# Attention feeding an ELU feed-forward layer on one core: W1 loaded by column group, unit 1's v cast moved off GpSimd, units 4 and 5 turned by DMA

## The chip, the cores and the metric

The kernel runs on one core of a Trainium2 chip. The metric is device time in microseconds (us) of one execution. TensorE (PE) multiplies, VectorE (DVE), ScalarE (ACT) and GpSimd (POOL) do elementwise work, SyncE (SP) issues DMAs. POOL and ACT can issue DMAs too; a DMA issued by POOL runs in another queue (q0 in the profile) than one issued by SP (q1).

## The reference

Inputs are q, k and v of shape (8, 8, 576, 64), `w_in` (512, 2048) and `w_out` (2048, 512), all float32.

```python
q_s = softmax(q, axis=-1)            # over the 64 features of a row
k_s = softmax(k, axis=2)             # over the 576 positions
kv  = einsum('bhsd,bhse->bhde', k_s, v)
x   = einsum('bhsd,bhde->bhse', q_s, kv)      # -> (8*576, 8*64) = (4608, 512)
h   = x @ w_in                                # (4608, 2048)
g   = where(h > 0, h, exp(min(h, 0)) - 1)     # ELU
out = g @ w_out                               # (4608, 512)
```

## The kernel before

**Units and blocks.** The attention is cut into 16 units n: batch n // 2, and four of its eight heads. The rows of x are cut into 9 blocks j of 512 rows. For every block, GEMM1 (line 541) makes 2048 columns of h in 8 groups g of 256 (8 matmuls of 128x512 each, called H j.g here), the ELU makes G j.g from it, and GEMM2 (line 586) makes four output tiles ts of 128 rows (16 matmuls each; O j.ts[a:b] is a part of them). That is 576 + 576 matmuls.

**One unit.** Loads of q, k, v (576 KB each). `stage1`: exp of q and of k on ACT (lines 355, 359), cast of v to bf16 (line 363 on POOL or line 366 on ACT), then on DVE the row sums of exp q (371), their reciprocal (375) and the scaled QS (379). QS has to be turned: `tp` does it with 9 PE transposes (402) and a copy to qsT on ACT (409) or DVE (412); `turn` and `widen` do it with a DMA transpose issued by SP (418) into QT and an ACT copy to qsT (430). `kv_mm` is 36 small bf16 matmuls (454), for one unit or, with two columns of PSUM, for two units in a row; `m` divides by the sum of exp k (463) and writes MBLK (467). `ao_mm` (485) makes x transposed in two parts ao n.0 and ao n.1, and `xt` copies it into XT (507 on ACT, 510 on DVE). With `BYDMA = 6` units 0 to 5 go through `tp`; with `CASTS = 6` v of units 1 to 5 is cast on POOL.

**ELU.** ACT takes exp of a PSUM tile (557; E j.g). In blocks 0 and 1 odd groups take relu on ACT (568; R j.g) and one DVE operation (570); even groups, and all later ones, take two DVE operations (574 and 576). The result is GT. GEMM1 alternates between two PSUM tiles, so H j.(g+2) has to wait until G j.g was made.

**Order.** Operations are collected with their reads and writes, which give the semaphore waits. The order in which each engine issues its own operations is not planned at run time: it is written out as lists of operation numbers in `ORDER` (one list for each of PE, ACT, DVE, POOL and SP), and every engine keeps to its list. An operation that waits holds up everything behind it on its engine; a DMA that waits holds up every later DMA of its queue.

**Head.** SP loads q0, q1, k0, v0, k1, v1. POOL then loads W1 in six DMAs: 1024 columns in halves of the contraction (units 0, 1 give half each of it), then the other 1024 columns. The first of them waits for v0 (`gate`). The cast of v1 stands in POOL's list between the fifth and the sixth. W2 and the loads of units 2 to 5 follow on POOL. The matmuls of line 651 are fillers, which no result needs.

**Shared storage.** GT of block 1 lies over QS, qsT, v of odd early units and over block 0's output tiles OSBX (line 276), so G 1.6 and G 1.7 have to wait until the stores of block 0 have left. QT is a single buffer.

Decoded, the lists of before start like this (T = transposes on PE, vc = cast of v, ms = memset, D-transposes are `turn`):

```
PE   T0a kv0 T0b ao0.0 T1a T1b kv1 H0.0(half 0) ao1.0 H0.1(half 0) H0.0(half 1) ... H0.7 O0.0 O0.1 ...
ACT  expq0 expq1 expk0 vc0 expk1 qsT0a qsT0b qsT1a xt0.0 xt1.0 E0.0 E0.1 R0.1 E0.2 ...
DVE  ms ID, ms RZK, sum0 rec0 ms MBLK1, QS0, ms VB0, sum1 ms MBLK0, rz0 M0 ms VB1, rec1 M0 QS1 xt0.0 rz1 qsT1b M1 M1 xt1.0
POOL W1 x5, vc1, W1, W2.0 W2.1 q2 k2 v2 W2.2 q3 k3 v3 vc2 W2.3 q4 v4 vc3 q5 k4 vc4 v5 k5 vc5
SP   q0 q1 k0 v0 k1 v1, q6 st0.0 v6 st0.1 st0.0 st0.3 q7 st0.1 k6 k7 st0.3 st0.2 st0.2 v7 ...
block 1, PE   H1.0 H1.1 T4 H1.2 O1.1 O1.0 kv4 H1.3 ao4.0 ... ao4.1+kv5 H1.4 T5 ... ao5.1 H1.7 ... H2.0 ... H2.1 O1.0 kv6+kv7 O1.1 O1.2
block 1, ACT  expq4 .. expq5 E1.0 expk4 E1.1 R1.1 qsT4 E1.2 expk5 expq6 xt4.0 E1.3 xt4.1 R1.3 vc6 E1.4 qsT5 E1.5 R1.5 xt5.0 E1.6 expk6 E1.7 R1.7 expq7 expk7 xt5.1 vc7 E2.0 osb1.0 E2.1
```

Of the kernel before, what the change touches and what calls it, by code (L numbers as in the profile page):

```python
# [16 lines left out]
NU = 2 * B  # L17
CH = 9
BYDMA = 6
CASTS = 6  # L20
# [3 lines left out]
        "26 30 28 44 40 42 47 64 51 65 67 68 66 69 79 83 90 100 112 125 126 134 87 133 128 127 104 "  # L24
        "146 136 106 135 147 149 123 148 131 129 153 137 154 156 143 150 155 169 181 185 192 207 206 "
        "187 208 196 219 218 212 220 224 236 237 235 243 241 261 245 249 263 267 244 262 269 268 282 "
        "288 273 308 323 292 359 286 312 296 316 364 328 330 324 374 334 338 355 399 360 368 407 391 "
        "372 375 379 395 447 415 400 452 417 422 439 411 418 487 443 462 448 456 460 479 467 463 505 "
        "483 488 503 527 495 510 499 506 535 540 531 550 548 536 566 544 551 555 574 581 570 618 589 "
        "575 591 623 585 596 592 610 614 649 619 633 627 634 631 641 645 654 664 638 658 650 671 679 "  # L30
        "675 662 665 684 692 680 688 697 669 693 701 705 718 710 714 706 731 736 723 719 727 757 732 "
        "740 744 749 753 745 770 762 758 766 775 783 771 779 784 788 789 793 797 801 "),
    "act": (
        "3 20 31 21 22 32 27 29 41 45 52 70 73 74 76 80 81 84 91 92 101 94 113 88 114 95 89 105 116 "
        "124 117 130 132 157 173 166 144 151 160 163 198 170 174 182 183 186 193 199 226 197 209 213 "
        "210 228 221 225 238 239 242 246 227 264 265 252 253 250 254 270 289 283 309 251 293 349 287 "
        "301 299 313 297 298 329 317 331 321 325 300 320 335 365 339 356 348 361 404 382 369 373 384 "
        "408 392 376 380 381 433 396 383 405 401 416 432 423 470 412 453 419 440 444 449 457 461 480 "
        "472 464 469 492 468 484 493 489 504 471 496 521 511 500 528 520 507 541 532 559 537 558 560 "
        "549 545 552 557 582 605 571 556 567 579 590 576 580 624 586 597 593 604 615 611 620 628 632 "  # L40
        "635 642 646 659 655 651 640 672 639 676 666 663 681 685 689 698 702 694 711 707 715 737 720 "
        "670 728 733 724 741 750 754 746 759 763 767 772 776 780 785 790 794 798 802 804 "),
    "dve": (
        "0 2 23 24 7 25 4 34 5 37 38 6 35 39 36 46 48 43 49 50 53 71 72 75 77 78 82 85 86 93 102 97 "
        "103 98 99 115 119 120 107 108 109 121 138 139 140 145 152 176 177 178 201 171 172 184 188 "
        "194 189 190 202 195 203 214 215 216 211 222 223 229 230 240 231 247 248 266 255 256 257 271 "
        "272 274 284 275 276 277 278 279 285 294 295 302 303 314 315 304 350 318 319 351 326 327 336 "
        "352 337 340 357 358 341 362 342 363 343 344 370 345 371 385 386 377 378 387 434 397 402 398 "
        "435 424 403 425 426 473 413 414 436 427 428 474 420 429 421 445 446 450 451 458 475 459 465 "
        "466 490 485 486 491 522 512 513 523 501 514 524 515 502 508 516 509 517 533 534 538 539 561 "  # L50
        "546 547 553 554 572 562 573 563 577 606 578 598 587 599 588 607 594 595 616 600 601 608 602 "
        "603 617 621 622 629 630 647 648 636 637 660 661 652 653 677 678 667 668 682 683 690 691 703 "
        "695 696 704 708 709 716 717 721 722 729 730 734 742 743 735 755 747 748 756 760 761 768 769 "
        "773 774 781 782 "),
    "gp": (
        "1 14 15 16 17 18 33 19 54 55 56 57 58 59 60 61 62 96 63 110 122 118 141 111 175 180 142 200 "),
    "sp": (
        "8 9 10 11 12 13 179 159 205 162 158 168 204 161 191 217 167 165 164 234 233 232 260 259 310 "
        "280 311 291 258 307 290 281 305 333 347 306 322 366 346 332 354 353 409 390 388 393 389 367 "
        "394 431 441 406 455 437 410 438 478 454 430 476 442 482 494 519 518 481 477 529 497 525 498 "  # L60
        "526 565 530 542 584 568 543 569 625 564 609 583 626 612 643 644 613 656 673 657 674 699 686 "
        "687 700 712 738 726 713 739 725 777 778 751 752 764 765 795 786 787 791 796 792 800 803 799 "),
# [178 lines left out]
class Gen:  # L241
# [49 lines left out]
    def init(self):  # L291
        S = self.S
        S.add("dve", 100, lambda e: e.memset(self.ID[:, :], 0.0), -95, W=["ID"])
        S.add("gp", 300, lambda e: e.affine_select(
            self.ID[:, :], self.ID[:, :], compare_op=ALU.not_equal, fill=1.0, base=0,
            pattern=[[-1, 128]], channel_multiplier=1), -38, X=["ID"])
        self.ident = S.ops[-1]
        S.add("dve", 60, lambda e: e.memset(self.RZK[0][:, :], 0.0), -90, W=["RZK0"])
        S.add("act", 1400, lambda e: e.activation(self.RZK[0][:, :], self.RZK[0][:, :], AF.Exp), -80,
              X=["RZK0"])  # L300
        self.table = S.ops[-1]
        for i in range(2):
            S.add("dve", 150, lambda e, i=i: e.memset(self.VB[i][:, :, :, D:D + 1], 1.0), -8,
                  W=[f"VBone{i}"])
            S.add("dve", 300, lambda e, i=i: e.memset(self.MBLK[i][:, :, :].bitcast(F32), 0.0), -8,
                W=[f"MBLK{i}", f"MBLK{i}0", f"MBLK{i}1"])

    def load(self, n, t, key, eng="gp", follow=None):
# [6 lines left out]
        chain = eng == "gp" and n < 4  # L315
        S.add(eng, ISSUE[eng], lambda e: e.dma_start(dst, src), key, W=[name],  # L316
              dma=f"{name}{eng}", nbytes=128 * 4608, follow=self.gpq if chain else follow)
        S.ops[-1].margin = 400 if n < 4 else 1000 if n < 6 else 1500
        if chain:
            self.gpq = S.ops[-1]  # L320
# [7 lines left out]
    def load_w1(self, two, half, key, after=()):  # L328
        w = self.w_in.rearrange("(h kc d) f -> h d kc f", h=2, d=D)
        sl = slice(two * 1024, (two + 1) * 1024)  # L330
        ks = slice(0, 4) if half is None else slice(2 * half, 2 * half + 2)
        xs = (0, 1) if half is None else (half,)
        for h in range(2):
            self.S.add("gp", ISSUE["gp"], lambda e, h=h: e.dma_start(  # L334
                self.W1[h:128:2, ks, sl], w[h, :, ks, sl]), key,
                W=[f"W1_{s}{x}{h}" for x in xs for s in (2 * two, 2 * two + 1)],
                dma=f"w1{two}{xs[0]}{h}", nbytes=len(xs) << 19, after=after, follow=self.gpq)
            self.gpq = self.S.ops[-1]

    def load_w2(self, s, key, after=()):  # L340
# [4 lines left out]
        self.gpq = self.S.ops[-1]  # L345
        return self.gpq

    def stage1(self, n, key, vconv="gp", what="qk"):
# [8 lines left out]
        if "k" in what:  # L357
# [4 lines left out]
            if vconv == "gp":  # L362
                S.add("gp", 1053, lambda e: e.tensor_copy(  # L363
                    VB[:, :, :, 0:D], v[:, :, :, :]), key - 50, R=[vname], W=[f"VB{i}"])
            else:
                S.add("act", t_act(1152, False), lambda e: e.activation(  # L366
                    VB[:, :, :, 0:D], v[:, :, :, :], AF.Copy), key - 50, R=[vname], W=[f"VB{i}"])
            self.conv = S.ops[-1]
        if "q" not in what:
# [4 lines left out]
            key - 3, R=[f"qR{i}"], W=[f"ZQ{i}"])  # L374
# [69 lines left out]
    def kv_mm(self, n, ps, at=KV):  # L444
# [12 lines left out]
        return 510 if at == self.KV else 280, [f"kR{i}", f"VB{i}", f"VBone{i}"], mm  # L457
# [390 lines left out]
```

## Time and profile before

| | before |
|---|---|
| median of 13 runs | 305.58 us (305.18 to 307.09) |
| the profiled execution, its own time | 305.43 us |
| its span, first to last instruction | 303.6 us |
| PE busy | 288.3 us, 95% of the span |
| DVE, ACT busy | 189.5 us (62%), 180.6 us (59%) |
| POOL busy | 21.6 us (7%) |
| moved by DMA | 49.37 MB, 163 GB/s on the mean |

The span is what the rows of the profile lie in; 1.8 us of the execution's own time lie outside it. A row of the timeline is start, length, engine, line, operation, output<-inputs, shape and count; in brackets stands the idle time before it and what ended it. PE rows are pipelined: the length of a row overlaps the next one, so the cost of a piece of PE work is read from start to start. A matmul of 128x512 costs 0.227 us that way (16 of them from 106.11 to 109.74).

### The profile page before, as it was taken

Reading aid. Unit: us, or ns where it says so; the run is one execution under the profiler, and the core shown is the slowest. Engines: PE = TensorE matmul, PEld = TensorE weight load, DVE = VectorE, ACT = ScalarE, POOL = GpSimd, SP = SyncE. Lnnn points to the kernel's source line nnn. Section 1 sums busy time; section 2 is a strip of 40 time slices with the busy share of each in tenths; the row PEclk is TensorE's granted clock in tenths of the full one; section 3 lists DMA queues with packets and bytes.
Section 4 is the critical chain, followed back from the end, with each engine's and each line's share of the span. In section 5 each row is a group of like instructions: output and inputs, shape, how many; then the busy total and the mean of one; then the engine's idle time right before and its main releaser. Section 6 shows DMA issues by size and latency. Waiting matters only on the chain.

```text
span 303.6 us, 4456 instructions
## 1 busy us (share of the span) xinstructions
PE 288.3 (95%) x1875; PEld 234.9 (77%) x1875; DVE 189.5 (62%) x243; ACT 180.6 (59%) x210; POOL 21.6 (7%) x32
## 2 busy tenths in 40 slices
PE   0699999999999999999999999999999999999994
PEld 0577877778788888888888888878888888888883
DVE  2849854988959777598478657574755435644400
ACT  5658749998978859754975675634534234423411
POOL 0770235100000000000000000000000000000000
PEclk9999999999999999999999999999999999999999
DMA  7999997859677394837779122242020300200424
GB/s 268 367 377 393 390 383 250 282 143 304 182 225 217 121 332 119 219 73 203 197 226 314 45 96 56 54 92 54 17 52 0 71 17 17 69 2 0 104 54 119
DMA packets 32371, 49.37 MB, mean 163 GB/s; under 512 B 13920, under 2 KB 13920, under 8 KB 32352
## 3 DMA queue, kind: packets, MB, share of 16 engines
q1 hardware_dynamic: 27312, 33.50, 38.9%
q0 software_dynamic: 4960, 15.47, 15.3%
q8 instruction: 14, 0.23, 0.3%
q10 hardware_dynamic: 80, 0.13, 0.1%
q14 instruction: 5, 0.04, 0.0%
HBM read 36.70 MB, written 9.44 MB: 152 GB/s over the span
## 4 chain that ended last, share of the span: by engine, by line
PE 88%; DMA 6%; POOL 1%; DVE 1%; ACT 1%; SPq 0%; issue 0%
PE PS L586 42%; PE PS L541 41%; DMA W<-in_moe_w_in_dram 4%; PE PS L485 3%; DMA VR<-in_v_dram 2%; PE PS L454 2%; POOL W L334 1%; PE PS L402 1%; SPq L316 0%; DVE QS L379 0%; DVE GT L576 0%; POOL VB L363 0%; ACT ESB L557 0%; DVE MBLK L467 0%; DVE ESB L574 0%
## 5 line engine op out<-in xcount | busy, mean ns | idle before, releaser
L541 PE MATMUL PS<-XT,W 128*128 128x512 f32 x576 | 140.9, 393 | 0.9 <-ACT XT L507 0.6
L586 PE MATMUL PS<-W,GT 128*128 128x512 f32 x576 | 140.6, 392 | 0.0
L541 PEld LDWEIGHTS PS<-XT,W 128*128 128x128 f32 x576 | 106.2, 188 | 24.7 <-ACT XT L507 1.0
L586 PEld LDWEIGHTS PS<-W,GT 128*128 128x128 f32 x576 | 106.9, 188 | 22.5 <-ACT OSB L603 0.4
L557 ACT ACTIVATE ESB<-PS 128x1024 f32<-128x1024 f32 x72 | 73.6, 1027 | 69.2 <-PE PS L541 69.0
L574 DVE TENSOR_SCALAR ESB<-ESB 128x1024 f32<-128x1024 f32 x64 | 44.1, 691 | 66.4 <-ACT ESB L557 66.2
L576 DVE TENSOR_TENSOR GT<-ESB,PS 128x1024 fp32r<-128x1024 f32 x64 | 77.6, 1218 | 1.7
L603 ACT ACTIVATE OSB<-PS 128x512 f32<-128x512 f32 x32 | 19.0, 596 | 29.2 <-PE PS L586 20.7
L371 DVE TENSOR_REDUCE ZQ<-QR 128x18 f32<-128x1152 f32 x16 | 21.6, 1348 | 10.9 <-ACT QR L355 10.8
L507 ACT ACTIVATE XT<-PS 128x512 fp32r<-128x512 f32 (+6 forms) x32 | 19.4, 609 | 10.8 <-PE PS L485 10.6
L379 DVE TENSOR_TENSOR QS<-QR,RZQ 128x1152 f16<-128x1152 f32 x16 | 23.1, 1441 | 0.3
L355 ACT ACTIVATE QR<-QR 128x1152 f32<-128x1152 f32 x16 | 18.7, 1167 | 2.8 <-DMA QR<-in_q_dram 2.8
L359 ACT ACTIVATE KR<-KR 128x1152 bf16<-128x1152 f32 x16 | 18.5, 1161 | 0.7 <-DMA KR<-in_k_dram 0.7
L402 PE MATMUL PS<-ID,QS 128*128 128x128 f16 x54 | 4.7, 235 | 10.3 <-DVE QS L379 10.3
L485 PE MATMUL PS<-qsT,MBLK 128*128 128x320 f32 (+5 forms) x64 | 14.0, 306 | 0.0
L485 PEld LDWEIGHTS PS<-qsT,MBLK 128*128 128x128 f32 x64 | 11.5, 189 | 2.9 <-ACT XT L507 0.6
L366 ACT ACTIVATE VB<-VR 128x1152 bf16<-128x1152 f32 x11 | 12.8, 1164 | 0.3 <-DMA VR<-in_v_dram 0.3
L430 ACT ACTIVATE qsT<-QT 128x1152 fp32r<-128x1152 f16 x10 | 11.7, 1166 | 1.7 <-PE PS L454 1.7
L402 PEld LDWEIGHTS PS<-ID,QS 128*128 128x128 f16 x54 | 3.3, 104 | 11.8 <-DVE QS L379 10.7
L570 DVE SCALAR_TENSOR_TENSOR GT<-PS,ESB 128x1024 fp32r<-128x1024 f32 x8 | 9.8, 1224 | 3.1 <-ACT ESB L568 2.7
L467 DVE TENSOR_TENSOR MBLK<-PS,RZK 64x128 fp32r<-64x128 f32 x32 | 9.2, 288 | 0.8
L463 DVE RECIPROCAL RZK<-PS 128x2 f32<-128x2 f32 x16 | 2.6, 165 | 10.0 <-ACT XT L507 5.4
(27 smaller groups left out, 67.5 us busy)
## 6 DMA issues: line engine op xcount, KB each, us to landing
out_dram<-OSB SPq DMA_DIRECT2D x63, 128.0 KB, 2.4
QR<-in_q_dram SPq DMA_DIRECT2D x12, 576.0 KB, 4.4
KR<-in_k_dram SPq DMA_DIRECT2D x12, 576.0 KB, 5.0
VR<-in_v_dram SPq DMA_DIRECT2D x12, 576.0 KB, 4.2
W<-in_moe_w_out_dram POOLq DMA_DIRECT2D x4, 1024.0 KB, 14.6
QR<-in_q_dram POOLq DMA_DIRECT2D x4, 576.0 KB, 12.6
KR<-in_k_dram POOLq DMA_DIRECT2D x4, 576.0 KB, 11.4
VR<-in_v_dram POOLq DMA_DIRECT2D x4, 576.0 KB, 13.7
```

Of the source, the lines that this page charges most:

```text
L355: S.add("act", t_act(1152, False), lambda e: e.activation(flat(q), flat(q), AF.Exp), key - 3, X=[f"qR{i}"], follow=self.table)
L359: S.add("act", t_act(1152, False), lambda e: e.activation(ek[:, :, :, :].rearrange("p h c d -> p (h c d)"), flat(k), AF.Exp), key - 2, X=[ ...
L371: S.add("dve", t_dve(1152), lambda e: e.tensor_reduce(self.ZQ[i][:, :, :].rearrange("p h c -> p (h c)"), q[:, :, :, :].rearrange("p h c d ...
L379: S.add("dve", t_dve(1152), lambda e: e.tensor_tensor(qso, q[:, :, :, :], rz, ALU.mult), key - 3, R=[f"qR{i}", f"RZQ{i}"], W=[f"QS{self.al ...
L485: last = e.matmul(P[:, y:y + n_], M[:, f, :], T[:, c0:c1, f * 64:f * 64 + 64], start=True, stop=True)
L507: S.add("act", t_act((h1 - h0) * n_, True), lambda e, dst=dst, src=src: e.activation(dst, src, AF.Copy), key, W=W, X=X)
L541: last = e.matmul(P[:, t * 512:(t + 1) * 512], self.W1[:, kc, tt * 128:(tt + 1) * 128], self.XT[:, kc, rc:rc + BLK], start=(kc == 0), stop ...
L557: S.add("act", t_act(1024, True), lambda e: e.activation(esb[:, :], P[:, :], AF.Exp), key, W=[f"E{i}"], X=banks)
L574: S.add("dve", t_dve(1024, 2), lambda e: e.tensor_scalar(esb[:, :], esb[:, :], 1.0, -1.0, ALU.min, ALU.add), key, X=[f"E{i}"])
L576: S.add("dve", t_dve(1024), lambda e: e.tensor_tensor(gt, esb[:, :], P[:, :], ALU.max), key, R=[f"E{i}"], W=gw, X=banks)
L586: last = e.matmul(dst, GT[:, jj, ts * 128:(ts + 1) * 128], self.W2[:, jj, :], start=(jj == 0), stop=(jj == 15))
L603: S.add("act", t_act(512, True), lambda e: e.activation(osb[:, :], src, AF.Copy), key, W=[f"O{i}0", f"O{i}1"], X=[f"b{bk}"])
```

## The change

`load_w1` takes a range of groups: W1 comes in eight DMAs, groups 0 to 2 (768 columns) in two halves of the contraction, groups 3 and 4 (512 columns), groups 5 to 7 (768 columns). The first of them wait for k0 in place of v0 (`gate`). W2 no longer waits for the cast of v1. The cast of v1 is made of two halves, one on ACT (line 366's kind) and one on DVE. Memsets of VB and MBLK come first on DVE. With `BYDMA = 4` units 4 and 5 are turned by DMA and widened on ACT; with `CASTS = 4` their v is cast on ACT. k-v of units 4 and 5 is one pair. The first two groups of block 1's GEMM1 are issued in halves of the contraction. All five lists of `ORDER` are written anew. The diff without the lists:

```diff
-BYDMA = 6
-CASTS = 6
+BYDMA = 4
+CASTS = 4
+CAST0, CAST1 = "act", "split"
@@ init
         for i in range(2):
-            S.add("dve", 150, lambda e, i=i: e.memset(self.VB[i][:, :, :, D:D + 1], 1.0), -8,
-                  W=[f"VBone{i}"])
-            S.add("dve", 300, lambda e, i=i: e.memset(self.MBLK[i][:, :, :].bitcast(F32), 0.0), -8,
-                W=[f"MBLK{i}", f"MBLK{i}0", f"MBLK{i}1"])
+            S.add("dve", 80, lambda e, i=i: e.memset(self.VB[i][:, :, :, D:D + 1], 1.0), -88,
+                  W=[f"VBone{i}"], follow=S.ops[-1] if i else None)
+            S.add("dve", 280, lambda e, i=i: e.memset(self.MBLK[i][:, :, :].bitcast(F32), 0.0), -88,
+                  W=[f"MBLK{i}", f"MBLK{i}0", f"MBLK{i}1"], follow=S.ops[-1])
@@ load_w1
-    def load_w1(self, two, half, key, after=()):
+    def load_w1(self, g0, g1, half, key, after=()):
         w = self.w_in.rearrange("(h kc d) f -> h d kc f", h=2, d=D)
-        sl = slice(two * 1024, (two + 1) * 1024)
+        sl = slice(g0 * 256, g1 * 256)
...
@@ stage1
-            if vconv == "gp":
-                S.add("gp", 1053, lambda e: e.tensor_copy(
-                    VB[:, :, :, 0:D], v[:, :, :, :]), key - 50, R=[vname], W=[f"VB{i}"])
-            else:
...
+            for eng, h0, h1, x in {"gp": [("gp", 0, 2, "")], "act": [("act", 0, 2, "")],
+                                   "dve": [("dve", 0, 2, "")],
+                                   "split": [("act", 0, 1, ""), ("dve", 1, 2, "x")]}[vconv]:
...
@@ program
-            if (n, t) == (0, "v"):
+            if (n, t) == (0, "k"):
                 gate = S.ops[-1]
-        for two, half in ((0, 0), (0, 1), (1, None)):
-            self.load_w1(two, half, -30, [gate, self.ident] if (two, half) == (0, 0) else ())
+        for g0, g1, half in ((0, 3, 0), (0, 3, 1), (3, 5, None), (5, 8, None)):
+            self.load_w1(g0, g1, half, -30, [gate, self.ident] if half == 0 else ())
             S.ops[-2].behind = loaded
-        self.stage1(0, -8, vconv="act")
+        self.stage1(0, -8, vconv=CAST0)
-        self.stage1(1, -5)
+        self.stage1(1, -5, vconv=CAST1)
-        after = [self.conv]
-        self.load_w2(0, -29, after)
-        self.load_w2(1, -29, after)
+        self.load_w2(0, -29)
+        self.load_w2(1, -29)
...
+        def batch(b):
+            n = 2 * b
+            if b == 2:
+                yield from (first(n), loads(("v", n + 1), ("q", n + 2)), first(n + 1, "k"),
+                            loads(("v", n + 2)), wide(n), kv2(n), loads(("k", n + 2), ("k", n + 3)))
+            else:
+                yield from (first(n, "q"), loads(("q", n + 2)), wide(n))
...
+        for half in range(2):
+            for g in range(2):
+                self.hg_mm(1, g, 2 if g == 0 else g % 2, key, half)
         for g in range(8):
-            self.hg(1, g, 2 if g == 0 else g % 2, key, "da"[g % 2])
+            self.hg(1, g, 2 if g == 0 else g % 2, key, "da"[g % 2], g > 1)
```

The new lists, decoded in the same way (vcA, vcD are the halves on ACT and DVE):

```
PE   T0b T0a kv0 T1b T1a ao0.0 kv1 H0.0(half 0) ao1.0 H0.1(half 0) H0.0(half 1) ... H0.7 ao0.1+ao1.1 O0.1 O0.2 O0.3 O0.0 ...
ACT  expq0 expq1 expk0 vc0 qsT0b qsT0a expk1 vcA1 qsT1a xt0.0 xt1.0 E0.0 E0.1 R0.1 E0.2 ...
DVE  ms VB0, MBLK0, VB1, ID, MBLK1, RZK, sum0 rec0 QS0 sum1 rec1 QS1 rz0 M0 M0 vcD1 qsT1b xt0.0 rz1 M1 M1 xt1.0
POOL W1 x8, W2.0 W2.1 q2 k2 v2 q3 W2.2 W2.3 v3 k3 vc2 q4 v4 vc3 q5 k5 k4 v5
SP   q0 q1 k0 v0 k1 v1, st0.3 st0.0 q6 D-transpose4 v6 st0.1 D-transpose5 st0.2 st0.2 q7 v7 st0.0 st0.1 st0.3 k7 k6 q8 D-transpose6 ...
block 1, PE   H1.1, H1.0 (half 0), H1.0, H1.1 (half 1), H1.2 O1.1[0:2] O1.0[0:4] H1.3 O1.1[2:4] kv4+kv5 O1.1[4:6] H1.4 H1.5 O1.0[4:6] ao4.0 O1.1[6:8] H1.6 O1.1[8:10] ao4.1 H1.7 O1.0[6:8] ao5.0 O1.0[8:10] O1.1[10:12] O1.0[10:12] H2.0 O1.1 O1.0 H2.1 ao5.1+kv6+kv7 O1.2
block 1, ACT  expq4 osb0.2 osb0.3 xt3.0 xt3.1 vc4 expq5 E1.0 E1.1 R1.1 expk4 E1.2 vc5 expk5 E1.3 R1.3 widen4 E1.4 vc6 E1.5 R1.5 xt4.0 E1.6 xt4.1 widen5 E1.7 xt5.0 R1.7 expq6 vc7 expk7 expk6 osb1.0 E2.0 E2.1
block 1, DVE  sum4 rec4 QS4 m1.0 G1.0 G1.1 sum5 m1.2 G1.2 rec5 QS5 rz4 G1.3 M4 M4 rz5 M5 m1.4 M5 G1.4 G1.5 m1.6 G1.6 G1.7 sum6 ...
```

## The prediction

> **What bounds the kernel now.** I read the page's first and fourth part, then the chain of waits in order of time up to 60 us, then the timeline of its pieces.
>
> ```profile
> PE 288.3 (95%) x1875; PEld 234.9 (77%) x1875; DVE 189.5 (62%) x243; ACT 180.6 (59%) x210; POOL 21.6 (7%) x32
> ...
> PE 88%; DMA 6%; POOL 1%; DVE 1%; ACT 1%; SPq 0%; issue 0%
> ```
>
> PE is the bound: from its first GEMM matmul at 16.91 to its end it has hardly an idle row. The 1152 GEMM matmuls at 0.227 us (start to start, 16 of them from 106.11 to 109.74) are 261 us and are not touched. What can be won is the head before 16.91, other PE work, and restarts of PE.
>
> ```profile
> 2.27 6.93 DMA VR<-in_v_dram
> 9.20 0.30 issue
> 9.50 3.25 POOL W L334 x5
> 12.75 1.05 POOL VB L363
> 13.80 11.49 DMA W<-in_moe_w_in_dram
> 25.29 0.04 issue
> 25.33 7.55 PE PS L541 x32
> ```
>
> The chain says: v0 lands at 9.20, POOL issues five W1 loads, then casts v1, and only then issues the sixth, which lands at 25.29 and starts the second half of GEMM1. But PE idled just 0.15 us for it. The start at 16.91 has another cause, which the timeline shows:
>
> ```profile
> 12.49 2.64 DVE L379 TENSOR_TENSOR QS<-QR,RZQ 128x1152 f16<-128x1152 f32 x1
> 12.71 1.19 POOL L363 CAST VB<-VR 128x1152 bf16<-128x1152 f32 x1
> 15.18 0.68 PE L402 MATMUL PS<-ID,QS 128*128 128x128 f16 x9 [1.20 <-DVE QS L379]
> 15.67 0.70 ACT L409 ACTIVATE qsT<-PS 128x640 fp32r<-128x640 f16 x1 [2.70 <-PE PS L402]
> 16.27 0.59 ACT L507 ACTIVATE XT<-PS 128x512 fp32r<-128x512 f32 x1
> 16.91 1.19 PE L541 MATMUL PS<-XT,W 128*128 128x512 f32 x4 [0.64 <-ACT XT L507]
> ```
>
> QS of unit 1 takes 2.64 us beside POOL's cast, against 1.36 at 44.10, where POOL is idle; PE, then ACT, then the copy to XT follow one another. The DMA has a hole in the same place:
>
> ```profile
> 11.00:12.50 1.50, 1.50 (x44) 1.43 (x33) 0.95 (x6) 1.50 (x3) 1.50 (x3) 1.00 1.05 319
> ...
> 14.00:17.00 3.00, 1.18 (x46) 0.96 (x46) 2.49 (x4) 1.19 (x2) 3.00 (x5) 1.00 0.93 280
> 17.00:25.30 8.30, 8.18 (x34) 6.14 (x34) 4.76 (x8) 4.72 (x6) 4.00 (x6) 1.00 1.19 409
> ```
>
> (The last column is GB/s: 280 beside the 409 that it can do.)
>
> **The head.** Removed: the cast on POOL, and the memsets between DVE's steps. They now run from 0.8 to 1.7, when DVE has nothing (its first input is there at 5.89), and cost nothing; ID is ready near 1.9, and W1 isn't asked for before 7.7. DVE by its rows: QS of unit 0 ends at 8.85 (9.03 before), sums of unit 1 take 1.33, the reciprocal 0.25, QS 1.36: it ends near 11.85 instead of 15.13. Then MBLK of unit 0 (0.17 + 0.3 + 0.3) to 12.6, ao0.0 on PE near 12.75 to 13.3. ACT: the two qsT copies after vc0, to 11.6, exp k1 to 12.7.
>
> What comes last now is v1: its half casts stand on ACT ahead of qsT1a and xt0.0, on DVE ahead of qsT1b and xt0.0, and kv1 on PE ahead of H0.0. All three engines stand behind its landing. In the trace it has landed by 12.2 (its last packets at 11.7). The first W1 packet there comes at 11.3, 1.8 us after its issue at 9.50, so the two queues hardly ever ran together. With the gate at k0, whose exp starts at 7.72, POOL issues from 8.0 (0.3 after the landing, as in the chain's row), and W1's packets start near 9.8. Then 0.68 MB of k1 and v1 are still to come (1.75 us at 387 GB/s).
>
> Here a rule speaks against the change. If W1 were served behind what was queued earlier, v1 would still land at 12.2: half casts to 13.3, qsT1 to 13.95, xt0.0 to 14.6, H0.0 at 14.75, a gain of 2.15 us. The Trainium skill, "DMA: Bandwidth & Descriptors", section "Queues, rings and completion order", says that each DMA engine goes round the queues that have work, a packet from each. The trace has 0.4 us of overlap (11.3 to 11.7), in which packets of both queues alternate, as the rule says. Rows of W1 are now 3072 bytes, those of v 2304: v gets 43% of 395 GB/s, 0.68 MB take 4.0 us, v1 lands near 14.25. Then: half casts (0.6, half of 1.17) to 14.9, qsT1a (0.65) to 15.5, xt0.0 (0.6 on ACT, 0.69 on DVE) to 16.2, H0.0 near 16.25. Gain 0.65. I take this, since rule and overlap agree. If W1 gets more than its share (two thirds), v1 lands at 15.2 and 0.4 us is lost. Ends of the head: -2.15 to +0.4, value -0.65.
>
> W1 itself: its eight issues at 0.65 us fill the hole, and 4.87 MB from 9.8 at 405 GB/s land by 22.3, not 25.29. The groups of 768 columns need 0.79 MB per half. None of them is later than PE asks; the 0.15 us goes.
>
> **Block 1.** The parts removed from PE, by start to start:
>
> ```profile
> 55.27 0.68 PE L402 MATMUL PS<-ID,QS 128*128 128x128 f16 x9
> 55.76 2.07 PE L541 MATMUL PS<-XT,W 128*128 128x512 f32 x8
> ...
> 80.47 0.78 PE L454 MATMUL PS<-VB,KR 64*64 64x65 bf16 x72
> 81.18 3.06 PE L586 MATMUL PS<-W,GT 128*128 128x512 f32 x12
> ```
>
> Nine transposes are 0.49 us, and the matmul after them is late by 0.09: 2 x 0.58 = 1.15. A single k-v is 0.42 (58.88 to 59.30) and its restart 0.13, two are 1.10; the pair is 0.71 + 0.13. Saved 0.25. Together 1.4 us of PE work. The DMA transposes come in its place: SP issue 1.6 us, landing 4 to 5 us later (73.57 to 78.48 for unit 6), the widening copy costs ACT what the copy from PSUM did.
>
> ACT pays. In these windows (fourth busy column: ACT) it has little left:
>
> ```profile
> 51.50:57.80 6.30, 6.30 (x35) 4.86 (x34) 6.13 (x7) 6.09 (x8) 1.15 (x1) 1.00 0.78 259
> 57.80:66.40 8.60, 8.60 (x112) 6.44 (x112) 7.28 (x12) 8.51 (x10) 0.00 (x0) 1.00 0.58 182
> 66.40:82.10 15.70, 15.70 (x139) 12.70 (x139) 13.28 (x14) 14.44 (x16) 0.00 (x0) 1.00 0.78 232
> ```
>
> 29.0 of 30.6 us. The casts of v4 and v5 add 2 x 1.06 (78.61 to 79.67); the two osb copies that lay at 51.32 mostly come earlier. I walked the new lists from H1 at 50.9 (51.51 less the head), with intervals of 1.06 for exp, cast and widening, 0.92 for E, 0.96 for R, 1.22 for G. ACT is then dense. PE waits for G1.0 before O1.1 (0.4), for G1.1 (0.3), for G1.3 before H1.5 (0.2; it stands behind rz4 and so behind kv4+kv5), for G1.4 before H1.6 (0.4): 1.3, and 0.4 of restarts. The same stretch before (H1.0 at 51.51 to O1.2 at 82.15, 30.6 us) holds 112 matmuls (25.4), T, k-v and ao (1.15 + 1.10 + 1.1 + 0.85), so 1.05 of waits. Change: -1.4 + 0.65 = -0.75.
>
> Loads that moved: k5 and k4 wait for kv3 on POOL, v5 for v4's cast; they land near 52.5, 54 and 57, casts and exps ask at 56.7 or later. Block 1 by halves is the same matmuls; H1.0 had not waited before: nothing. D-transpose 5 waits on SP for QS5 and for widen4 (QT), near 64, and holds st0.2, q7, v7, st0.0, st0.1, st0.3, k7, k6 behind it. G1.6 may write only after st0.0 and st0.1: these land near 72.5, G1.6 ends at 73.9, H2.0 asks at 74.2. Covered by 0.3; if the cover goes, each us costs one. Everything after block 2 is the same work in another order; before has about 0.3 us of true waits there, I take 0, with +-0.4.
>
> **Sum.** 305.43 (own time of the profiled execution) - 0.65 - 0.75 = 304.0; the median stands 0.15 above it, so 304.15, say 304.1.
>
> **Rivals.**
> First, W1 doesn't delay v1: head -2.15, block 1 the same: 302.6. For it: SP's loads were all issued by 4.08. Against: the alternating packets, and the rule.
> Second, slower, and the mechanism is ACT in block 1. It is 95% busy, gets 2.1 us more, and its list is fixed: if casts wait (v5, k4) or E waits in line behind them, GEMM1's PSUM tiles come free late and each us of ACT is one of PE. All 2.1 us and the 1.05 of margin lost on PE, less 1.4 and 0.65: +1.1, 306.5. It decides once PE's waits in that stretch pass 3.1 us (1.05 + 1.4 + 0.65). For it: my walk has ACT end E2.0 2.2 us after PE ends H2.0. Against: GEMM2 work lies between, which takes that up.
> Third, the gains are given back by a late D-transpose or by v1 at 15.2: 305.0 to 305.9, no change that can be seen.
>
> **How the numbers follow.** A measurement of this kernel can tell about 0.2%, 0.6 us. Likeliest case 304.1: 0.46; no delay of v1, 302.6: 0.24; given back: 0.14; ACT: 0.16. So faster 0.70, same 0.14, slower 0.16. The range leaves out most of ACT's case and the rest below 302.3: 302.3 to 305.9.
>
> **What would show it.** The first row of line 541 near 16.25 (14.75: first rival; over 16.9: the head failed), half casts on ACT and DVE starting near 14.3; QS of unit 1 in 1.4 us; no wait of PE for W1; 36 instead of 54 transposes of line 402 on PE, 12 DMA transposes; ACT without a gap from 51 to 80; H1.5 and H1.6 late by some tenths; O1.2 near 80.7. I am wrong if PE waits over 3 us between H1 and O1.2, or in G1.6 for a store.

## The result, and the profile after

The kernel after takes 303.02 us (median of 11 runs, 302.45 to 303.82), the kernel before 305.86 us on the same chips (median of 48). The ratio is 0.9909, with a 95% interval of 0.9898 to 0.9921: 0.9% faster, 1.1 us more than forecast and inside the range. The profiled execution of after takes 303.24 us, its span is 301.4. Two of the ten runs of one kernel below (e11) fell in a slower state, at a granted clock of 0.988, and are left out of its figures.

The first and the fourth part of its page answer to those shown of before. PE has 1.4 us less to do, and the chain still consists of PE to 87%; DVE and SP's queue (SPq) now have some per cent of it, most of it in block 1, as will be seen.

```profile
PE 286.9 (95%) x1845; PEld 234.1 (78%) x1845; DVE 188.8 (63%) x244; ACT 183.2 (61%) x213; POOL 20.5 (7%) x31
...
PE 87%; DMA 6%; DVE 3%; SPq 2%; ACT 1%; issue 0%
```

The timeline of the head (start, length, engine, line, operation; in brackets the idle time before it and what ended it; lines after 541 have moved by 4, so GEMM1 is line 545 and GEMM2 line 590):

```profile
8.60 5.08 POOL L335 DMA_DIRECT2D W<-in_moe_w_in_dram  x8 [6.74 <-DMA KR<-in_k_dram]
10.72 1.36 DVE L383 TENSOR_TENSOR QS<-QR,RZQ 128x1152 f16<-128x1152 f32 x1
12.84 0.76 DVE L371 CAST VB<-VR 128x576 bf16<-128x576 f32 x1
13.01 0.68 ACT L368 ACTIVATE VB<-VR 128x576 bf16<-128x576 f32 x1
14.59 0.69 DVE L514 CAST XT<-PS 128x512 fp32r<-128x512 f32 x1 [0.26 <-PE PS L489]
15.33 1.21 PE L545 MATMUL PS<-XT,W 128*128 128x512 f32 x4 [0.37 <-DVE XT L514]
```

QS of unit 1 is back at 1.36 us. The half casts of v1 start at 12.84 and 13.01, and GEMM1 at 15.33 in place of 16.91. Where the span's 2.2 us came from, by five marks in each trace (start of GEMM1 in block 0; of GEMM1 in block 1, H1; of O1.2 in GEMM2, when 32 matmuls of GEMM2 lie behind H1; of the last matmul; the end):

| us | before | after | gained in this stretch |
|---|---|---|---|
| GEMM1 of block 0 starts | 16.91 | 15.33 | 1.58 |
| H1 | 51.51 | 49.44 | 0.49 |
| O1.2 | 82.23 | 80.51 | -0.35 |
| the last matmul starts | 299.11 | 297.44 | -0.04 |
| end of the span | 303.63 | 301.44 | 0.51 |

(The prediction has O1.2 of before at 82.15. Its first matmul, the fifth behind the k-v at 81.18, starts at 82.23.)

The head gave well over twice what the prediction had, block 1 lost time where a gain of 0.75 was forecast, and the two errors partly cancelled. The experiments take the two apart. The last half microsecond lies behind PE's work: three stores follow the last copy in before, two in after. First before, then after:

```profile
299.54 0.60 ACT L603 ACTIVATE OSB<-PS 128x512 f32<-128x512 f32 x1 [2.47 <-PE PS L586]
300.16 1.11 SPq L613 DMA_DIRECT2D out_dram<-OSB  x2
300.17 0.54 ACTq L613 DMA_DIRECT2D out_dram<-OSB  x1
```
```profile
297.86 0.60 ACT L607 ACTIVATE OSB<-PS 128x512 f32<-128x512 f32 x1 [0.67 <-PE PS L590]
298.49 0.48 SPq L617 DMA_DIRECT2D out_dram<-OSB  x1
298.49 0.55 ACTq L617 DMA_DIRECT2D out_dram<-OSB  x1
```

### The profile page after: what moved, and what is told of

Read it like the earlier page. It is cut to its first block, busy times and chain, and to the rows that moved or that the text cites. A ratio compares the mean times of both kernels' runs of the same rounds, so it can differ in the third digit from the quotient of the medians.

```text
span 301.4 us, 4403 instructions
## 1 busy us (share of the span) xinstructions
PE 286.9 (95%) x1845; PEld 234.1 (78%) x1845; DVE 188.8 (63%) x244; ACT 183.2 (61%) x213; POOL 20.5 (7%) x31
## 4 chain that ended last, share of the span: by engine, by line
PE 87%; DMA 6%; DVE 3%; SPq 2%; ACT 1%; issue 0%
PE PS L590 42%; PE PS L545 39%; PE PS L489 3%; DMA QT<-QS 2%; DMA out_dram<-OSBX 2%; PE PS L458 2%; DMA QR<-in_q_dram 1%; DVE QS L383 1%; PE PS L406 1%; DVE ZQ L375 1%; SPq L318 1%; PE PS L655 1%; SPq L617 1%; DVE XT L514 1%; SPq L422 0%; DVE GT L580 0%
## 5 line engine op out<-in xcount | busy, mean ns | idle before, releaser
L383 DVE TENSOR_TENSOR QS<-QR,RZQ 128x1152 f16<-128x1152 f32 x16 | 21.7, 1356 | 1.6 <-DMA QT<-QS 1.2
L368 ACT ACTIVATE VB<-VR 128x1152 bf16<-128x1152 f32 (+1 forms) x14 | 15.9, 1136 | 1.3 <-DMA VR<-in_v_dram 1.2
L489 PE MATMUL PS<-qsT,MBLK 128*128 128x320 f32 (+5 forms) x64 | 14.2, 308 | 0.0
L434 ACT ACTIVATE qsT<-QT 128x1152 fp32r<-128x1152 f16 x12 | 13.9, 1161 | 0.3 <-DMA QT<-QS 0.3
L489 PEld LDWEIGHTS PS<-qsT,MBLK 128*128 128x128 f32 x64 | 11.8, 194 | 2.8 <-ACT XT L511 0.4
L406 PE MATMUL PS<-ID,QS 128*128 128x128 f16 x36 | 3.7, 266 | 9.2 <-DVE QS L383 9.2
L406 PEld LDWEIGHTS PS<-ID,QS 128*128 128x128 f16 x36 | 2.9, 122 | 9.7 <-DVE QS L383 9.2
L572 ACT ACTIVATE ESB<-ESB 128x1024 f32<-128x1024 f32 x8 | 8.5, 1060 | 0.2
```

The costliest lines, as they stand in the source:

```text
L383: S.add("dve", t_dve(1152), lambda e: e.tensor_tensor(qso, q[:, :, :, :], rz, ALU.mult), key - 3, R=[f"qR{i}", f"RZQ{i}"], W=[f"QS{self.al ...
L489: last = e.matmul(P[:, y:y + n_], M[:, f, :], T[:, c0:c1, f * 64:f * 64 + 64], start=True, stop=True)
```

## Experiments

Medians stand with the lowest and highest run, ratios (to the kernel before on the same chip) with their 95% interval. In the kernels of e1, e2 and e5 to e10, where `ORDER` is written on fewer lines, every line number is 36 lower than in after: GEMM1 is L509, GEMM2 L554, k-v L422. A profile is of one run. Those of e2 and e8 were 0.8 us above their median, that of e4 0.7 below, so that their ends are not to be set against each other. The marks of all profiles, in us (v1: its landing; W1: the first of POOL's issues of W1 and the landing of the last one; block 1: from H1 to O1.2):

| | v1 | W1 issued, landed | GEMM1 starts | H1 | O1.2 | block 1 | end |
|---|---|---|---|---|---|---|---|
| before | 12.18 | 9.50, 25.29 | 16.91 | 51.51 | 82.23 | 30.7 | 303.6 |
| after | 12.81 | 8.60, 24.53 | 15.33 | 49.44 | 80.51 | 31.1 | 301.4 |
| after, again (e12) | 12.69 | 8.48 | 14.88 | 49.26 | 80.43 | 31.2 | 301.3 |
| e1 head only | 12.79 | 8.57 | 15.45 | 49.50 | 80.87 | 31.4 | 302.2 |
| e2 block only | 12.48 | 9.81, 25.89 | 17.20 | 51.95 | 83.46 | 31.5 | 304.4 |
| e3 no gate | 19.79 | 2.17 | 21.94 | 57.45 | 88.79 | 31.3 | 309.6 |
| e4 gate v0 | 12.24 | 9.55, 25.26 | 15.63 | 50.12 | 81.76 | 31.6 | 302.7 |
| e8 gate v0, v1 on ACT | 12.75 | 10.13, 26.40 | 15.65 | 52.11 | 83.49 | 31.4 | 304.5 |
| e11 gate q1 | 14.11 | 6.70 | 16.26 | 50.36 | 82.11 | 31.8 | 303.0 |
| e5 turn 4 first | 12.57 | 8.37 | 15.13 | 49.15 | 82.03 | 32.9 | 303.0 |
| e6 stores first | 12.54 | 8.34 | 15.38 | 49.45 | 80.07 | 30.6 | 300.9 |
| e7 both | 12.44 | 8.23 | 15.09 | 49.10 | 79.93 | 30.8 | 300.9 |
| e9 casts on POOL | 12.07 | 7.87 | 15.26 | 49.31 | 80.64 | 31.3 | 301.5 |
| e10 casts on POOL, stores first | 12.11 | 7.91 | 15.05 | 49.15 | 79.56 | 30.4 | 301.1 |

### The two halves of the change alone (e1, e2)

e1 is the new head with the block 1 of before; e2 is the old head (W1 in six loads behind v0, v1 cast on POOL, memsets where they were) with the new block 1. Lists are ordered to match.

```diff
# e1, against after
-BYDMA = 4
-CASTS = 4
+BYDMA = 6
+CASTS = 6
# e2, against after
-CAST0, CAST1 = "act", "split"
+CAST0, CAST1 = "act", "gp"
-            if (n, t) == (0, "k"):
+            if (n, t) == (0, "v"):
-        for g0, g1, half in ((0, 3, 0), (0, 3, 1), (3, 5, None), (5, 8, None)):
+        for g0, g1, half in ((0, 4, 0), (0, 4, 1), (4, 8, None)):
```

> Kernel before with the head of the change alone: W1 by groups with the gate at k0, v1's cast split over ACT and DVE, memsets first; block 1 and everything behind it as before (units 4, 5 turned on PE, their v cast on POOL). Theory A (the gain is made ahead of block 1 and block 1 gives some back): H0.0 near 15.3 as in the changed kernel, H1 near 49.4, block 1 then at its own length of before (30.6 us from H1 to O1.2), so 0.4 to 0.7 us less than the changed kernel there: median near 303.2 to 303.6, ratio to before 0.991 to 0.993, as much as the whole change or nearly. Theory B (the prediction's sum: head 0.65, block 1 0.75): ratio 0.998.

> Kernel before with the block 1 part alone: units 4, 5 turned by DMA and widened on ACT, their v cast on ACT, k-v of 4, 5 as a pair, block 1's first groups in halves, the new lists from block 0's ELU on; the head (W1, gate, v1 on POOL, memsets) as before. Theory A: H0.0 at 16.9 as before, block 1 longer by about 0.4 us, what lies behind it shorter by about 0.5: ratio 0.998 to 1.001. Theory B (the prediction: 1.4 us of PE work saved, 0.65 of waits added): ratio 0.9975 with block 1 shorter by 0.75 us.

Measured: e1 303.81 us (303.53 to 304.07), ratio 0.9943 (0.993 to 0.9957). e2 305.31 us (304.83 to 306.15), ratio 0.9997 (0.9987 to 1.0007). So the head alone is worth 0.6%, the block part alone nothing, and both together 0.9%. The marks say how they combine. Behind the early head even the old block 1 gets longer, from 30.7 us to 31.4 in e1, 0.53 of it a wait that before has not:

```profile
56.35 1.20 PE L554 MATMUL PS<-W,GT 128*128 128x512 f32 x4 [0.53 <-DVE GT L544]
```

So the 0.35 lost in the table above is 0.65 that the early head costs block 1, less 0.3 that the new block wins there (31.1 against 31.4); behind the old head the new block costs 0.8 (31.5 in e2, by the profile of its slowest run). The half microsecond at the end comes with the block part: from the start of the last matmul to the end it is 4.51 us in before and 4.48 in e1, 4.01 in after and 4.00 in e2.

### Does W1 take DMA time from v1? (e3, e4, e11)

The gate says which load has to land before POOL issues W1. Three other places, on after:

```diff
# e3: no gate
-            self.load_w1(g0, g1, half, -30, [gate, self.ident] if half == 0 else ())
+            self.load_w1(g0, g1, half, -30, [self.ident] if half == 0 else ())
# e4: gate at v0
-            if (n, t) == (0, "k"):
+            if (n, t) == (0, "v"):
# e11: gate at q1
-            if (n, t) == (0, "k"):
+            if (n, t) == (1, "q"):
```

> The changed kernel with W1's loads freed of the gate: POOL issues them from about 2 us on, while SP's six loads are still being issued. Round robin between the queues: v1 shares from the first microseconds, lands near 17 instead of 12.8, H0.0 near 19, time up by 3 us or more. Drain (a DMA engine takes no packet of W1 while it has packets of the other queue): first W1 packets at 11.3 all the same, v1 at 12.8 or earlier, H0.0 at 15.3 or earlier, time within 0.5 us of the changed kernel. Order of arrival: W1 issued at 2.0 to 4 comes ahead of k1 and v1, v1 lands 1 to 3 us later, H0.0 at 16.5 to 18.

> The changed kernel with the gate at v0, as before the change. Drain or order of arrival: v1 lands as in the changed kernel, the first W1 packets come about 0.4 us later (issue at 9.5 to 10.1, 1.8 us on), H0.0 unchanged at 15.3, W1 has room, so the same time within 0.3 us. Round robin would make v1 land earlier than with the gate at k0, by up to 0.6 us, and H0.0 with it.

> The changed kernel with W1's gate at q of unit 1, landed near 6.2: POOL issues from 6.5. Round robin from the moment the descriptors are there (1.8 us after the issue, 8.3): v1 lands near 16.4, H0.0 near 18.6, 3 us lost. Fetched ahead (a DMA engine first serves what it had fetched of the other queue; without the gate W1's first packet came 4.2 us after its issue, about 0.9 MB of q, k, v after its descriptors were there): first packets near 10.7, v1 at 13.4, H0.0 at 16, 0.5 to 1 us lost. Drain: first packets at 11.3, v1 at 12.2 to 12.8, no loss.

Measured: e3 312.07 us (311.43 to 314.65), ratio 1.023 (1.0193 to 1.0267); e4 305.14 (304.45 to 306.27), 0.9993 (0.9981 to 1.0006); e11 304.62 (303.27 to 306.91), 0.9971 (0.9945 to 0.9997).

The cleanest measure of what W1 costs v1 is the time between the landings of k0 and v1, the last 1.77 MB of SP's queue: 12.18 - 7.69 = 4.49 us before, 12.81 - 8.30 = 4.51 after. W1 cost v1 0.02 us, although its loads were issued 4.2 us before v1 was down. That v1 is 0.63 later than before is there already at k0 (0.61), when no W1 load had been issued. It is the last of the sixteen DMA engines: the first has written its completion of v1 at 11.28 in after and 11.30 in before, the last at 12.34 and 11.71. Kernels with the same head have v1 at 12.07 (e9) to 12.81; why one engine lags in some executions stays open.

With the gate at q1 the same stretch takes 14.11 - 8.18 = 5.93 us, and ACT waits for v1:

```profile
14.13 0.68 ACT L368 ACTIVATE VB<-VR 128x576 bf16<-128x576 f32 x1 [1.13 <-DMA VR<-in_v_dram]
```

Without a gate it is the prediction's fear in full. v1 lands at 19.79, and PE stands behind v0 and then v1 (k-v of units 0 and 1, then the first row of GEMM1):

```profile
15.08 0.71 PE L458 MATMUL PS<-VB,KR 64*64 64x65 bf16 x36 [3.94 <-ACT VB L368]
...
20.64 0.48 PE L458 MATMUL PS<-VB,KR 64*64 64x65 bf16 x36 [1.96 <-DVE VB L371]
21.94 1.75 PE L545 MATMUL PS<-XT,W 128*128 128x512 f32 x4 [0.82 <-DVE XT L514]
```

(By its record e3's clock also fell to half from 22.35 to 25.76, so not all of its 9 us are v1's delay.)

The packets say when the sharing begins. In e3, from 11 to 15 us, each microsecond moves 69 to 73 packets of W1 and 76 to 80 of SP's loads: one for one, the rule of the Trainium skill ("DMA: Bandwidth & Descriptors", "Queues, rings and completion order": a DMA engine goes round the queues it has work for). But the first packet of W1 comes 4.2 us after the first issue there (2.17 to 6.33) and in e11 4.1 us (6.70 to 10.83), 2.7 us in after (8.60 to 11.29). In after, e1 and before it comes 6 to 9 ns behind the first engine's completion write for v1 (11.282 and 11.288 in after, 11.305 and 11.313 before). So the two kinds of packets that alternate from 11.3 to 11.7 before are not one engine going round two queues: they are engines that have finished v1 beside engines that have not. The counts agree: at 11.4, 11.5 and 11.6 us 5, 9 and 14 packets of W1 are under way in before, and 5, 10 and 13 engines are done with v1; in after 4, 10 and 11 packets, and 4, 9 and 11 engines. A queue that starts while another has work in hand is let in late: after 4.1 and 4.2 us in the two runs where the work in hand lasted that long, or sooner if the earlier queue has finished by then, as in after and before (with nothing left in its way it took 1.6 us, 10.13 to 11.70 in e8). With the gate at k0 v1's last packets fall inside that delay; with the gate at q1 they don't. What an engine does in that time isn't seen in a trace; that it first serves what it has already fetched of the earlier queue is a reading.

e4 shows the other side, a gate that is too late. v1 and the head are as quick as in after, but PE, now early, stands before W1:

```profile
15.63 1.16 PE L545 MATMUL PS<-XT,W 128*128 128x512 f32 x4 [1.17 <-DMA W<-in_moe_w_in_dram]
...
18.45 12.93 PE L545 MATMUL PS<-XT,W 128*128 128x512 f32 x55 [0.28 <-DMA W<-in_moe_w_in_dram]
```

The early head and the early W1 need each other: k0 is the one gate of the four that delays neither.

In after it is not v1 that GEMM1 starts behind. The chain of waits goes through PE, without a wait from 9.18 to 14.56 (L655 are fillers, L406 the transposes of unit 1, L489 is ao0.0):

```profile
11.92 0.97 PE PS L655 x8
12.89 0.96 PE PS L406 x9
13.85 0.71 PE PS L489 x2
14.56 0.02 issue
14.59 0.70 DVE XT L514
15.29 0.04 issue
15.33 1.21 PE PS L545 x4
```

PE is slow there. The nine transposes take 0.93 us (12.68 to 13.61), where nine took 0.49 in block 1 before:

```profile
12.68 1.17 PE L406 MATMUL PS<-ID,QS 128*128 128x128 f16 x9
13.61 0.94 PE L489 MATMUL PS<-qsT,MBLK 128*128 128x512 f32 x2
```

The trace's own record of the granted clock begins, at full clock, only at 14.12 us in after (the clock column of the views reads 1.00 ahead of it too, where nothing is recorded). All eight profiles of kernels with this head, gate at k0, in the order of that moment:

| us | v1 landed | full clock from | GEMM1 starts |
|---|---|---|---|
| e12 | 12.69 | 12.94 | 14.88 |
| e5 | 12.57 | 13.40 | 15.13 |
| e7 | 12.44 | 13.62 | 15.09 |
| e10 | 12.11 | 13.88 | 15.05 |
| after | 12.81 | 14.12 | 15.33 |
| e9 | 12.07 | 14.62 | 15.26 |
| e6 | 12.54 | 14.64 | 15.38 |
| e1 | 12.79 | 14.70 | 15.45 |

GEMM1's start goes with the clock and not with v1, whose earliest landing, in e9, goes with a late start. Only in e12, where the clock came first, does the chain lead back to v1; in e5, the next, it goes through DVE, in the six others through PE. In before the full clock was there at 12.69, well ahead of the transposes of unit 1 at 15.18. What sets the moment, and whether the fillers (eight run on to 12.68, while QS of unit 1 is ready at 12.08) help or hinder, no run here tries.

### What makes the hole in the DMA (e8)

The prediction had shown the hole of before (280 GB/s from 14 to 17) beside POOL's cast, which stood between W1's fifth and sixth load, and let the new issues fill it. e4 has no cast on POOL and has a hole all the same, but half of v1's cast is on DVE. e8 has v1 wholly on ACT:

```diff
# e8, against e4
-CAST0, CAST1 = "act", "split"
+CAST0, CAST1 = "act", "act"
```

> The changed kernel with the gate at v0 and unit 1's v cast whole on ACT, so that DVE makes no cast from SBUF to SBUF while W1's descriptors are written. Theory L (DVE's cast holds up POOL's descriptors; with the gate at k0 enough of them were written before): the hole in DMA from 13.5 to 14.8 (21 to 67 KB in a quarter of a us instead of 98) is gone or under half, W1's first half lands near 14.8 instead of 15.54, the second near 16.8 instead of 18.21; H0.0 near 15.6 because ACT's cast is 0.5 us longer; time nearer to the changed kernel than to that with the gate at v0, 303.3 to 304. Theory M (the hole comes from the late issue alone): same hole, 305.

Measured: 305.43 us (303.96 to 306.31), ratio 0.998 (0.9962 to 0.9998). The hole is there with no cast of v1 on POOL or DVE. In stretches of 2 us (busy time and count of PE, PEld, DVE, ACT, POOL, granted clock, DMA share, and GB/s in the last column) after, then e4, then e8:

```profile
13.00:15.00 2.00, 1.96 (x46) 1.46 (x44) 1.71 (x3) 1.81 (x4) 2.00 (x4) 1.00 1.16 384
15.00:17.00 2.00, 1.67 (x7) 1.40 (x8) 0.93 (x4) 0.18 (x1) 2.00 (x4) 1.00 1.24 386
```
```profile
13.00:15.00 2.00, 1.47 (x45) 0.99 (x43) 1.93 (x5) 1.33 (x3) 2.00 (x4) 1.00 1.03 227
```
```profile
15.00:17.00 2.00, 1.73 (x42) 1.43 (x42) 1.14 (x4) 0.30 (x1) 2.00 (x4) 1.00 1.02 285
```

e8 pays for it with PE's wait:

```profile
19.79 10.60 PE L509 MATMUL PS<-XT,W 128*128 128x512 f32 x45 [1.60 <-DMA W<-in_moe_w_in_dram]
```

What the runs show is a division by the moment of issue: between 13 and 17 us each kernel that issues W1 at 9.5 or later has 2 us of 227 to 285 GB/s (before 258, e2 240, e4 227, e8 285), and the ten that issue it by 8.6 have 350 to 413 throughout. e4 differs from after in the gate alone, so the later issue does bring the hole. By what way isn't settled.

### Where block 1 lost its gain (e5, e6, e7, e9, e10)

The chain of waits of after, in order of time, prints the loss (start, length, engine or queue, what):

```profile
51.94 1.37 DVE QS L383
53.31 0.02 issue
53.33 0.37 SPq L318
53.70 0.04 issue
53.75 7.39 DMA QT<-QS
61.14 0.02 issue
61.16 1.37 DVE QS L383
...
62.61 1.34 SPq L422
...
67.51 5.13 DMA out_dram<-OSBX
72.63 0.02 issue
72.66 1.23 DVE GT L580
73.89 0.04 issue
73.93 2.11 PE PS L545 x8
```

Read downwards: SP issues q6 and then the DMA transpose of unit 4, which lands only at 61.14. QS of unit 5 wants to write the buffer that this transpose reads, so DVE stands, and with it G1.3 behind it in DVE's list, which H1.5 waits for. SP issues the transpose of unit 5 behind it, and only then block 0's stores, which stand after it in SP's list; the last of them that matters lands at 72.63, and G1.6, which writes over its tile, ends at 73.89, where H2.0 starts. The waits of that stretch, by who waited for what (us in total, times, longest):

```profile
DVE GT L580 <- DMA out_dram<-OSBX: 1.8, 1, 1.8
...
DVE QS L383 <- DMA QT<-QS: 1.2, 1, 1.2
...
PE PS L545 <- DVE GT L574: 0.8, 1, 0.8
```

Two suspects, then: the stores behind transpose 5 (H2.0's wait, about 0.3 us: it starts 1.65 after the six matmuls at 72.28, where in e6 it is 1.37), and the chain of q6, transpose 4 and QS5 (H1.5's 0.8). e5 moves transpose 4 ahead of q6, e6 moves the stores ahead of transpose 5, e7 does both; e9 and e10 take ACT as the suspect and put the casts of v4 and v5 on POOL, e10 with the stores moved as well.

```diff
# SP's list, decoded. e5
-st0.3 st0.0 q6 D-transpose4 v6 ...
+st0.3 st0.0 D-transpose4 q6 v6 ...
# e6
-v6 st0.1 D-transpose5 st0.2 st0.2 q7 v7 st0.0 st0.1 st0.3 k7 k6
+v6 st0.1 st0.0 st0.1 st0.3 st0.2 st0.2 D-transpose5 q7 v7 k7 k6
# e7: both. e9, with vc4, vc5 moved to POOL's list (k5 k4 vc4 v5 vc5)
-vconv="gp" if n < CASTS
+vconv="gp" if n < 6
# e10: e9 and e6's list
```

> The changed kernel with one swap in SP's list: the DMA transpose of unit 4 ahead of the load of q6 (both become ready with QS4 at 53.3). Theory A (block 1 is set by the chain QS4, q6's load and transpose 4 in one queue, QS5 that may write the one QS buffer only when transpose 4 has read it, G1.3, H1.5; then transpose 5, the stores, G1.6, H2.0): transpose 4 lands near 59.6 instead of 61.14, QS5 starts when DVE is ready, at 60.0, PE's wait before H1.5 falls from 0.8 to 0.2 us or less, G1.6 waits 1 us less: 0.6 to 1.0 us less than the changed kernel, ratio to before 0.988. Theory B (ACT is the bound of block 1, with or without the transposes): H1.5 no earlier by more than 0.2 us, ratio 0.991 as the change.

> The changed kernel with the stores of block 0's output (st0.0, st0.1, st0.3, st0.2: five of eight) moved in SP's list ahead of the DMA transpose of unit 5, behind which they stand. SP idles there from 59.4 to 62.6, so transpose 5 is not later by more than 0.1 us. Theory A: G1.6 no longer waits for a store (1.8 us on DVE goes), H2.0 starts when GEMM2 before it ends, 0.3 to 0.5 us earlier, the wait before H1.5 stays 0.8: ratio 0.989 to 0.990. Theory B (ACT): G1.6 free, but H2.1 and what follows wait for ACT's E instead, nothing gained: 0.991.

> Both edits of SP's list at once. Theory A: block 1 from H1 to O1.2 in 30.0 us or less instead of 31.1; 1.0 us less than the changed kernel, ratio 0.987 to 0.988, median about 302.0. Theory B: 0.990 to 0.991.

> The changed kernel with v of units 4 and 5 cast on POOL again (CASTS of before for these two, the rest of the change kept): ACT loses 2.1 us of work between 50 and 59, POOL has nothing else there. Theory ACT (ACT is what PE's waits in block 1 lead back to, once or beside the transpose chain): G1.0 is not touched, E1.2, exp k5 and kv4+kv5 come 1 to 2 us earlier, PE's wait before H1.5 stays (it is QS5 behind transpose 4), the waits behind it shrink; 0.2 to 0.5 us less than the changed kernel, block 1 30.7 us. Theory T (only the transposes and stores in SP's list set it): block 1 within 0.15 us of the changed kernel's 31.1, no gain.

> The same with the five stores of block 0 ahead of unit 5's transpose. Theory ACT: both waits ease, block 1 in 30.2 us or less, 0.8 us or more less than the changed kernel: median near 302.2. Theory T: as the stores alone, block 1 30.6 us, 0.4 less than the changed kernel.

Measured: e5 304.72 us (303.88 to 306.66), ratio 0.9973 (0.9952 to 0.9995). e6 302.82, 0.9904 (0.9886 to 0.9922). e7 302.83, 0.9906 (0.9887 to 0.9925). e9 303.84 (303.33 to 305.89), 0.9943 (0.9924 to 0.9963). e10 302.66 (302.23 to 302.92), 0.9896 (0.9879 to 0.9912).

e5 takes H1.5's wait away: transpose 4 lands at 58.65. It is slower than after, because the stores now come later against PE (the one that G1.6 waits for lands at 74.15 in place of 72.63), and the wait comes back larger one step on. Of its waits and its timeline:

```profile
DVE GT L544 <- DMA out_dram<-OSBX: 3.8, 1, 3.8
```
```profile
75.45 2.11 PE L509 MATMUL PS<-XT,W 128*128 128x512 f32 x8 [2.17 <-DVE GT L544]
```

e6 takes away the other one. Block 1 falls from 31.1 to 30.6, H2.0 starts at 73.31 with no wait, and what is left is H1.5's 0.41. The ratio of e6, 0.9904, isn't clear of the 0.9909 of after. e7 removes H1.5's wait too and gains nothing over e6, where Theory A had a block 1 of 30.0 us or less: ACT is next in line, as kv4+kv5 waits for exp k5. First e6, then e7:

```profile
63.42 2.11 PE L509 MATMUL PS<-XT,W 128*128 128x512 f32 x8 [0.41 <-DVE GT L538]
```
```profile
59.82 0.78 PE L422 MATMUL PS<-VB,KR 64*64 64x65 bf16 x72 [0.43 <-ACT KR L323]
```

e9 relieves ACT and leaves the stores: the wait at H1.5 is gone, and H2.0 waits 0.95 for the store instead. Its text expected the wait at H1.5 to stay. It went because transpose 4, with the list of SP as in after, landed at 59.17 and not at 61.14 (v5's load, which no longer waits for ACT's cast, was issued at 50.11 and not at 51.66; that this made the difference isn't shown). So e9 doesn't show ACT to be a cause of that wait. e10 has both edits; of after's two waits of block 1 over 0.2 us only the 0.4 before O1.1 is left. First e9, then e10:

```profile
74.06 2.11 PE L509 MATMUL PS<-XT,W 128*128 128x512 f32 x8 [0.95 <-DVE GT L544]
```
```profile
72.79 2.00 PE L509 MATMUL PS<-XT,W 128*128 128x512 f32 x8
```

The last repeats after beside e9 and e10, on the same chip:

> The changed kernel once more, beside the others on the same chip: ratio to before 0.991, H0.0 at 15.1 to 15.4, block 1 31.1 us from H1 to O1.2. It is the measure for the runs with it.

Measured: 303.37 us (302.7 to 303.91), ratio 0.9922 (0.9905 to 0.9939). Its waits in block 1 are 0.38 before O1.1, 0.48 before H1.5 and 0.40 before H2.0, so single waits of after are good to some 0.3 us only. e9 isn't clear of it (0.9943 against 0.9922). e10 is 0.7 us below it (302.66 / 303.37 = 0.9977), the lowest median of all kernels here, and its intervals and after's overlap: probably better, by a quarter of a per cent, not shown beyond doubt. At O1.2 it is 0.95 us ahead of after, and gives 0.6 of that back later (221.5 us from there to the end against 220.9).

## Why the prediction was right, and where it was not

**The bound.** PE bounds, and the head before GEMM1 was where most could be won: of the span's 2.2 us, 1.6 came from there.

**The head: mis-sized, 0.65 against 1.58.** The step that failed is "Then 0.68 MB of k1 and v1 are still to come ... v gets 43% of 395 GB/s ... v1 lands near 14.25". It landed at 12.81, with W1 costing it 0.02 us. Two things were wrong in it: W1's first packet came 2.7 us after its issue, not 1.8 (which was the figure of before, where it had been waiting for v1 in the same way), and the alternating packets of before, taken as the evidence for sharing, were different engines. The first rival, "W1 doesn't delay v1", held: it had the start of GEMM1 at 14.75, two profiles of after have it at 15.33 and 14.88. What lies between is the clock of PE: ao0.0, which the prediction had at 12.75 to 13.3, came at 13.61 to 14.48 in after and set the 15.33. "All three engines stand behind its landing" fits the 14.88 alone. The rule that was weighed is not wrong: e3 and e11 show what it costs where it applies. The row against it was in the prediction too (k1 and v1 left, all issued by 4.08); it was given 0.24.

**The steps around it.** QS of unit 1 fell from 2.64 to 1.36 as worked out from the row at 44.10. The memsets moved at no cost. W1 was to fill the hole and land by 22.3: it landed at 24.53. The rate was 384 GB/s and more from 11.3 to 19, but it started 1.5 us later than assumed (11.29 for 9.8), and 0.9 MB of W2 came in ahead of its last packets. PE did not wait for it, so the 0.15 (with its restart 0.3) went, and that is most of what was gained between the start of GEMM1 and H1. That the hole comes from POOL's cast, as the prediction suggests, is not borne out: e8 has the hole without it.

**Block 1: wrong in sign, 0.35 lost against 0.75 gained.** What was removed from PE was right: 36 transposes of line 406 are left and 12 are by DMA, and k-v of units 4 and 5 is one pair. From start to start, what isn't GEMM takes 1.19 us less in this stretch. But its 112 GEMM matmuls take 28.46 us where they took 26.91, 1.55 more against the 0.65 forecast. The step that failed is "so 1.05 of waits": this was a remainder of a subtraction, and the trace of before lists no wait of PE over 0.2 us in this stretch. It held restarts, which stayed (a matmul behind a wait or a change of work takes some 0.1 us longer), and not waits that could be set against the new ones. The list of new waits, 1.3, is near what PE waited (1.17 in two of them), but by luck. The largest, 0.78 before H1.5, was given as 0.2: the walk had no wait of QS5 for transpose 4 (one QS buffer, 1.2 us of DVE), and let that transpose land 4 to 5 us after its issue, where it took 7.4. The waits for G1.1 and G1.4, 0.7 in the list, came to under 0.1. And e1 shows that the early head by itself costs block 1 0.65, for which the prediction has no term.

**The store and G1.6: right, but not as a cover.** "Land near 72.5, G1.6 ends at 73.9, H2.0 asks at 74.2" was measured as 72.63, 73.89 and 73.93. The 0.3 of cover was used up because PE reached H1 at 49.44, 1.5 us earlier than the walk had it; e6 shows that with the stores out of the way block 1 takes 0.45 less.

**The rest: 0.47 gained against 0,** just outside the +-0.4. It is not in PE's work, which is the same to 0.05 us from O1.2 to the last matmul, but in the stores behind it, 0.51, and it comes with the block part's lists (e2 has it, e1 hardly). "The same work in another order" did not ask which stores would be the last.

**The slower rival** (ACT in block 1, PE's waits over 3.1 us) did not come: PE's waits over 0.2 us there are 1.17 in all. ACT does set the next limit, as e7 shows, but behind two others.

## What to carry to other kernels

When the bound moves earlier, every cover that was priced in tenths (a store that lands 0.3 us ahead of its reader, weights that were 0.15 us late) has to be priced again from the new start, and all at once: here the earlier head with a late gate (e4) ran into W1, the early head alone (e1) brought block 1 a new wait, the block part alone (e2) gave nothing, and freeing one link of a chain (e5) made the next one worse. In a queue that waits in order, put what is ready and will be waited for (the stores) ahead of what has to wait (transpose 5): 0.45 us of block 1 in e6. And before two transfers are costed as sharing a rate, look at the landings, k0 to v1 here, and not only at packets of both kinds standing side by side. Where a start hangs on PE's first work, one profile is not enough: 0.45 us lay between two of one kernel.

## What was not expected of the hardware

A load on a second queue, issued while the first queue had work outstanding, moved its first packet 4.1 to 4.2 us after its issue (e11, e3), or as soon as an engine was done with the first queue (after, before). In after it cost v1 0.02 us; in e3, once let in, the two went one for one. The DMA transpose of unit 4 took 7.4 us to land in after (53.75 to 61.14), where it was issued behind a load, and 5.6 in e5, ahead of it (53.04 to 58.65); but behind the same load it took 5.6 in e9 as well, so the order isn't all of it. And between 13 and 17 us the DMA moved 384 GB/s where W1's issue began at 8.6, and for 2 us only 227 to 285 where it began at 9.5 or later, with no cast of v1 on POOL or DVE needed for it. The moment from which the record has PE at full clock moved by 1.8 us among executions of one head (12.94 to 14.70), and the start of GEMM1 by 0.57 with it.
